# Four output stores of the first chunk issued behind the next batch's query transposes

## The chip, the cores and the metric

The kernel runs on one core of a Trainium2 chip. The metric is device time in microseconds (us), the median of several runs. A core has five engines with instruction queues of their own: TensorE (PE in the profile; its weight loads are the row PEld), VectorE (DVE), ScalarE (ACT), GpSimd (POOL) and SyncE (SP). [...] In this kernel the transfers issued by SyncE and those issued by GpSimd are two separate queues.

## The reference

Eight batches of eight heads, 576 positions and 64 elements a head go through an attention whose softmaxes are taken apart: q is normalised over the head's elements, k over the positions, and the product of k and v is a 64x64 matrix per head. The result, 512 wide, goes through a layer norm and a two-layer network with a hidden width of 2048, and is added to it.

```python
q_s = exp(q - max(q, -1)); q_s /= sum(q_s, -1) + 1e-09
k_s = exp(k - max(k, 2));  k_s /= sum(k_s, 2) + 1e-09
kv = einsum('bhsd,bhse->bhde', k_s, v)
x = einsum('bhsd,bhde->bhse', q_s, kv)      # then to (8, 576, 512)
xn = (x - mean(x)) / sqrt(var(x) + 1e-06) * g_ln
out = x + maximum(xn @ w_ch1, 0) @ w_ch2    # w_ch1 512x2048, w_ch2 2048x512
```

## The kernel before

**Chunks.** The work is cut into nine chunks. Chunk c (0 to 7) is the first 512 of the 576 positions of batch c, as four tiles (t = 0 to 3) of 128 rows; position 4p + t lies on partition p of tile t. Chunk 8 (`C9`) holds the last 64 positions of all batches. For chunk c the network is run (`mlp_steps(c)`) while the attention of chunk c + 1 and the loads and exponentials of batch c + 2 go on beside it.

**Order.** The order of the instructions on each engine is written out by hand. `run(main, side)` goes through a list of TensorE steps with weights; a side task has a due place, and it is emitted when the sum of the weights gets there. So in chunk 1's list, `second_side()` (lines 857 to 880), a task at 9.3 comes ahead of one at 9.4, and on each engine the instructions stand in the order in which the tasks emit them. Each queue is executed in that order: an instruction that waits holds back all that stands behind it on its engine.

**The network.** Chunk 0 uses plain products (`mm1_part`, `mm2_stream`). From chunk 1 on the second layer, and from chunk 2 on the first layer too, uses seven products of half blocks in place of eight (`mm2_fast`, `mm1_fast`), with sums and differences of blocks prepared beforehand. For the first layer these are `tq`, four differences of blocks of the transposed, normalised chunk `xnT`. `sum_x` (lines 233 to 245) makes them on GpSimd in eight instructions, two for each of the four; the second needs the first, the fourth the second. TensorE uses the first in product 5, the second in product 6, the third in product 7 and the fourth in product 4 (line 716).

**Transposes.** `xnT` and `eqT` (the exponentials of q, transposed) are made by DMA transposes on SyncE's queue from batch 2 on (`dma_T`, line 253): `xn_T(2, 0, 2)` and `xn_T(2, 2, 2)` at 60 and 77 of chunk 1's list, `eq_T(2)` at 9.2, `eq_T(3)` at 85.

**Loads.** Batch b needs `qt`, `kt` (1 MB each), `ktr` (the last 64 keys, two small loads), `vt` and `vr`. Weights and the loads of batches 1 and 2 are issued by GpSimd, one behind the other (`load_behind`). From batch 3 on, q and k are issued by SyncE (`load_batch`, line 1063) and v by GpSimd (`load_v`, line 139), which also converts v to bf16 on the way. Batch 3's query load has one more dependency: `load_batch(3, (2,), eqTs[2][...])` at 9.3 of chunk 1's list has GpSimd copy four elements out of `eqT` of batch 2 into the place where `qt` will land (line 1070). The copy waits for the transposes of batch 2, and SyncE's load of `qt` waits for the copy; the `kt` load, the `ktr` loads and the transposes of chunk 2's `xn` stand behind it on SyncE's queue.

**Stores.** `y_out` (line 480) makes chunk 0's output rows on VectorE, one tile of 128x512 in fp32 at a time, in the buffer `ot` (four buffers), and issues the store to `out` on GpSimd at once (line 490), 256 KB each. Chunks 1 to 7 do the same in `y_quarter` (line 570, store at line 581).

On GpSimd's queue the order around the end of chunk 0 is thus: batch 2's loads, the four stores of chunk 0, the copy out of `eqT`, `load_v(3)`, then `sum_x(2)`.

Of the kernel before, what the change touches and what calls it, by code (L numbers as in the profile page):

```python
# [20 lines left out]
def kernel(  # L21
# [16 lines left out]
    nc = tc.nc  # L38

    B, H, S, D = q.shape  # L40
# [3 lines left out]
    T = 4  # L44
    SM = P * T
# [55 lines left out]
    def main_src(x, b, h0, hn):  # L101
        return x[b, h0 : h0 + hn, 0:SM, :].rearrange("h (p t) d -> p h (t d)", t=T)
# [19 lines left out]
    def load_krem(eng, b):  # L122
        for half in range(2):
            eng.dma_start(
                raws[b][3][SR * half : SR * half + SR],
                k[b, 4 * half : 4 * half + 4, SM:S, :].transpose([1, 0, 2]),
            )
# [3 lines left out]
    def cast_v(b, j, eng=None):  # L131
        hs = slice(4 * j, 4 * j + 4)
        dst = vm[:, b % 2, :, hs, 0:D].rearrange("p t h d -> p h t d")
        if eng is nc.scalar:
            nc.scalar.copy(dst, vts[b][:, hs])
        else:
            nc.vector.tensor_copy(out=dst, in_=vts[b][:, hs])

    def load_v(b):

        vts[b] = mlp.tile([P, H, T, D], BF16, tag="vt", name="vt", bufs=1)
        nc.gpsimd.dma_start(vts[b].rearrange("p h t d -> p h (t d)"), main_src(v, b, 0, H))
        if b == 1:
            load_krem(nc.gpsimd, b)
        for half in range(2):
            hs = slice(4 * half, 4 * half + 4)
            nc.gpsimd.dma_start(
                vr[SR * half : SR * half + SR, b % 2, hs, 0:D],
                v[b, hs, SM:S, :].transpose([1, 0, 2]),
            )  # L150
# [15 lines left out]
    def exp_k(b, j, hn=2):  # L166
        kt = raws[b][0]
        if j == 0:
            eks[b] = att.tile([P, T, H, D], BF16, tag="ek", name="ek", bufs=1)
        hs = slice(2 * j, 2 * j + hn)  # L170
        nc.scalar.activation(
            eks[b][:, :, hs, :].rearrange("p t h d -> p h t d"), kt[:, hs], AF.Exp
        )

    def prep_kvrem(b):
        nc.scalar.activation(ekr[:, b % 2], raws[b][3], AF.Exp)
# [9 lines left out]
    def exp_q(b, j, hn=2):  # L186
        if j == 0:
            new_eq(b)
        hs = slice(2 * j, 2 * j + hn)
        nc.scalar.activation(  # L190
            eqs[b][0][:, :, hs, :].rearrange("p t h d -> p h t d"),
            raws[b][2][:, hs], AF.Exp,
        )
# [11 lines left out]
    def reduce_q(c, t, tn=1):  # L205
        ts = slice(t, t + tn)
        nc.vector.reduce_sum(eqs[c][1][:, ts], eqs[c][0][:, ts], axis=AX.X)  # L207
# [49 lines left out]
    def eq_T(c):  # L257
        dma_T(eqTs[c], eqs[c][0].rearrange("p t h d -> p (t h d)"), 0, T)
# [103 lines left out]
    def kv_all(b):  # L362
        kv_mm(b, range(T + 1))
        kv_out(b)

    def start_x(c):
        xs[c] = (
            mlp.tile([P, T, DM], BF16, tag="x", name="x"),
            mlp.tile([P, T, 6], FP32, tag="st", name="st"),
            mlp.tile([P, T, DM], BF16, tag="xn", name="xn", bufs=1),  # L370
            mlp.tile([P, T, 2], FP32, tag="mv", name="mv"),
        )
        xnTs[c] = mlp.tile([P, T, KO1, P], BF16, tag="xnT", name="xnT")
# [21 lines left out]
    def square_sum(c, t):  # L395
        x, _, _, mv = xs[c]
        nc.scalar.activation(  # L397
            scrap, x[:, t], AF.Square, bias=mv[:, t, 0:1], scale=-float(DM),
            accum_out=mv[:, t, 1:2],
        )  # L400
# [26 lines left out]
    def rstd_op(c):  # L427
        mv = xs[c][3]
        lnv = sml.tile([P, T], FP32, tag="lnv", name="lnv")
        rstds[c] = mlp.tile([P, T], FP32, tag="rstd", name="rstd")  # L430
        nc.scalar.activation(
            lnv, mv[:, :, 1], AF.Ln, bias=eps_ln, scale=1.0 / DM ** 3
        )
        nc.scalar.activation(rstds[c], lnv, AF.Exp, scale=-0.5)
# [24 lines left out]
    def mm1_part(c, m, t0, tn, ko):  # L459
# [13 lines left out]
        if m % 2 == 1 and at + tn == 2 and ko == KO1 - 1:  # L473
# [3 lines left out]
            else:  # L477
                nc.scalar.activation(dst, ph, AF.Relu)

    def y_out(c, t, pc, cols=slice(0, 512), eng=None):  # L480
        if cols.start == 0:
            hbox["ot"] = outp.tile([P, DM], FP32, tag="ot", name="ot")
        ot = hbox["ot"][:, cols]
        nc.vector.scalar_tensor_tensor(
            ot, in0=pc, scalar=rstds[c][:, t : t + 1], in1=xs[c][0][:, t, cols],
            op0=ALU.mult, op1=ALU.add,
        )
        eng = eng or nc.gpsimd
        if c < B:
            eng.dma_start(  # L490
                out[c, 0:SM, :].rearrange("(p t) n -> p t n", t=T)[:, t, cols], ot
            )
        else:
            for half in range(2):
                eng.dma_start(
                    out[2 * t + half, SM:S, cols], ot[64 * half : 64 * half + 64]
                )

    def mm2(c, t, ko):
        if ko == 0:  # L500
            hbox["pc"] = mm_ps.tile([P, DM], FP32, tag="m", name="pc")
        nc.tensor.matmul(
            hbox["pc"], hbox["h"][:, ko, t, :], w2_sb[:, ko, :],
            start=(ko == 0), stop=(ko == KO2 - 1),
        )
        if ko == KO2 - 1:
            y_out(c, t, hbox["pc"])
# [12 lines left out]
    def quarter_w2(i, g):  # L520

        ks = slice(4 * g, 4 * g + 4)
        rows = [w2_sb[:, 8 * g + odd : 8 * g + 8 : 2, :] for odd in range(2)]
        (b11, b12), (b21, b22) = [(r[:, :, 0:DH2], r[:, :, DH2:DM]) for r in rows]
        t1, t2, t3, t4 = [w2_q[:, n, ks, :] for n in range(4)]
        dst, x, y = ((t1, b12, b11), (t3, b22, b12), (t2, b22, t1), (t4, b21, t2))[i]
        nc.vector.tensor_sub(out=dst, in0=x, in1=y)
# [312 lines left out]
    def recip_q(c):  # L840
        nc.vector.reciprocal(eqs[c][2], eqs[c][1])
# [15 lines left out]
    def second_side():  # L857

        s = [(p, lambda i=i: quarter_w2(i, 1)) for i, p in enumerate((13, 16, 44, 46))]
        s += [(8, lambda: xn_pT(1, 2, nc.scalar)), (12, lambda: xn_pT(1, 3, nc.vector))]  # L860
        s += [(3, lambda: exp_q(2, 0, 4)), (9, lambda: exp_q(2, 2, 4)), (9.2, lambda: eq_T(2))]
        s += [(42, lambda: square_sum(1, 2)), (67, lambda: square_sum(1, 3)), (71, lambda: rstd_op(1))]
        s += [(9.3, lambda: load_batch(3, (2,), eqTs[2][0:1, T - 1, NP - 1, 0:4])), (31, lambda: load_batch(3, (0,)))]
        s += [(18 + 2 * j, lambda j=j: cast_v(2, j)) for j in range(2)]
        s += [(9.4, lambda: load_v(3))]
        s += [(93 + j, lambda j=j: cast_v(3, j)) for j in range(2)]
        s += [(15 + 3 * t, lambda t=t: reduce_q(2, t, 2)) for t in (0, 2)]
        s += [(36, lambda: recip_q(2))]
        s += [(18, lambda: exp_k(2, 0, 4)), (22, lambda: exp_k(2, 2, 4)), (26, lambda: prep_kvrem(2))]
        s += [(41, lambda: kv_all(2))]  # L870
        s += [(46, lambda: start_x(2))]
        for t, (p0, p1) in enumerate(((52, 54), (57, 59), (62, 65), (70, 74))):
            s += spread([lambda t=t, i=i: po_mm(2, t, i) for i in range(NP)], p0, p1)
            s += [(p1, lambda t=t: x_fast(2, t)), ((73, 82, 88, 94)[t], lambda t=t: square_sum(2, t))]
        s += [(60, lambda: xn_T(2, 0, 2)), (77, lambda: xn_T(2, 2, 2)), (100, lambda: rstd_op(2))]
        s += [(75, lambda: exp_q(3, 0, 4)), (79, lambda: exp_q(3, 2, 4)), (85, lambda: eq_T(3))]
        s += [(97, lambda: exp_k(3, 0, 4)), (108, lambda: exp_k(3, 2, 4)), (113, lambda: prep_kvrem(3))]
        s += [(p, lambda i=i: sum_w1(i, 1)) for i, p in ((2, 28), (3, 30))]
        s += spread([lambda i=i: sum_x(2, i) for i in range(4)], 95, 108)
        return s  # L880
# [39 lines left out]
    def xn_pT(c, t, eng):  # L920
        pe_T(xnTs[c], xs[c][2][:, t], t, eng, None if c else g_col)
# [141 lines left out]
    def load_batch(b, parts=(2, 0), after=None):  # L1063

        alloc(b, parts)
        for which in parts:
            if after is None:
                nc.vector.memset(raws[b][which][0:1, 0, 0, 0:1], 0.0)
            else:
                nc.gpsimd.tensor_copy(out=raws[b][which][0:1, 0, 0, 0:4], in_=after)  # L1070
        for which in parts:
            load_main(nc.sync, b, which, 0, H)
        if 0 in parts:
            load_krem(nc.sync, b)
# [100 lines left out]
```

## Time and profile before

| | us |
|---|---|
| median of 3 runs | 265.17 |
| lowest, highest | 264.51, 265.96 |
| the profiled execution's own time | 264.17 |
| its span, first to last instruction | 261.9 |
| TensorE's matmuls busy | 255.9 (98%) |
| VectorE busy | 216.8 (83%) |
| ScalarE busy | 180.8 (69%) |
| GpSimd busy | 77.5 (30%) |

The profile is one execution. Its page gives busy times, the chain of work that ended last, and the costliest groups of instructions by line. The trace behind it answers further questions: time lines (start, duration, engine, line, what is written from what, and in brackets the idle time ahead with what ended it), waits (engine, line and the instruction waited for, total, number and longest), the time from a transfer's issue to its landing, and stretches (a stretch's length, then for PE, PEld, DVE, ACT and POOL the busy time and, in brackets, the number of instructions, then TensorE's granted clock, a measure of the DMA engines' load, and GB/s moved). PEq and SPq mean an engine's own queue of issues.

A store or load is "issued" when the engine hands it over; it "lands" when its completion is signalled. TensorE's matmuls are pipelined, so that the duration of one is longer than the distance to the next: 0.109 us for 256 columns.

### The profile page before, as it was taken

To read this page: it belongs to the slowest core of one execution; us is meant where nothing else is said; L and a number is where in the kernel's file an instruction comes from. 1 tells how busy PE (TensorE), PEld (TensorE's weight loads), DVE (VectorE), ACT (ScalarE), POOL (GpSimd) and SP (SyncE) were. 2 spreads that over 40 slices of the span, in tenths; PEclk is the share of its full clock that TensorE was granted. 3 is DMA by queue.
4 is the path that set the end of the run, shared out by engine and by line. 5 is a ranking of instruction groups with operands and counts; after the bars stand their busy time and mean duration, and the time that the engine had idled before them with its cause. 6 is when DMAs were issued, how large, how long until landed. Compare 5 with 4: busy or idle time off the path is not lost.

```text
span 261.9 us, 6813 instructions
## 1 busy us (share of the span) xinstructions
PE 255.9 (98%) x2700; PEld 217.5 (83%) x2700; DVE 216.8 (83%) x480; ACT 180.8 (69%) x356; POOL 77.5 (30%) x128
## 2 busy tenths in 40 slices
PE   8899999999999999999999999999999999999993
PEld 6689755766888998899889988998899888888883
DVE  5667777988889997989798979897989889977873
ACT  4787581897966788678867886788688378437400
POOL 8661237203049008500850085008200300030000
PEclk9999999999999999999999999999999999999999
DMA  6999999997987994899489969997805610421014
GB/s 220 255 202 206 336 218 301 286 165 234 210 151 230 298 145 87 239 290 142 86 247 284 139 86 253 276 146 142 260 5 78 176 73 1 83 95 68 0 43 120
DMA packets 69879, 45.00 MB, mean 172 GB/s; under 512 B 41492, under 2 KB 66072, under 8 KB 69848
## 3 DMA queue, kind: packets, MB, share of 16 engines
q0 software_dynamic: 20352, 22.29, 39.2%
q1 hardware_dynamic: 48896, 21.76, 39.0%
q10 hardware_dynamic: 600, 0.53, 0.6%
q8 instruction: 21, 0.34, 0.5%
q14 instruction: 10, 0.08, 0.1%
HBM read 36.70 MB, written 9.44 MB: 176 GB/s over the span
## 4 chain that ended last, share of the span: by engine, by line
PE 95%; DMA 2%; SPq 1%; ACT 0%; issue 0%; DVE 0%
PE ba L564 21%; PE bx L716 19%; PE bb L716 9%; PE ph L467 8%; PE bb L564 5%; PE be L564 5%; PE bc L564 5%; PE pc L513 5%; PE bc L716 5%; PE ph L452 3%; PE po L383 3%; DMA kt<-in_k_dram 2%; PE pkv L347 2%; PE ptr L900 1%; PE xt L320 1%; SPq L953 1%
## 5 line engine op out<-in xcount | busy, mean ns | idle before, releaser
L564 PEld LDWEIGHTS <-hs 128*128 128x128 bf16 x512 | 49.6, 98 | 5.6
L716 PEld LDWEIGHTS <-w_q 128*128 128x128 bf16 x448 | 43.2, 98 | 4.9
L564 PEld LDWEIGHTS <-hT 128*128 128x128 bf16 x392 | 37.4, 98 | 4.4
L245 POOL TENSOR_TENSOR tq<-xnT 128x256 bf16<-128x256 bf16 x20 | 12.9, 661 | 77.6 <-DMA xnT<-xn 46.4
L716 PEld LDWEIGHTS <-w1g 128*128 128x128 bf16 x336 | 32.2, 98 | 3.9
L564 PE MATMUL ba<-w_q,hs 128*128 128x256 bf16 x256 | 31.7, 273 | 0.0
L716 PE MATMUL bx<-tq,w_q 128*128 128x256 bf16 x224 | 29.0, 273 | 0.0
L581 POOL DMA_DIRECT2D out_dram<-ot x28 | 15.3, 555 | 46.0 <-DVE ot L575 46.0
L397 ACT ACTIVATE scrap<-x,mv 128x512 bf16<-128x512 bf16 x36 | 26.0, 721 | 1.8 <-DVE x L413 1.4
L413 DVE SCALAR_TENSOR_TENSOR x<-po,rq 128x512 bf16<-128x512 f32 x34 | 23.3, 686 | 1.4 <-PE po L383 1.2
L740 ACT COPY bc<-bx 128x512 f32<-128x512 f32 x28 | 15.2, 596 | 13.0 <-PE bx L716 13.0
L758 ACT ACTIVATE hT<-bc 128x512 bf16<-128x512 f32 x28 | 15.3, 595 | 12.2 <-PE bc L716 12.2
L747 DVE TENSOR_TENSOR bb<-bx,s 128x512 f32<-128x512 f32 x28 | 18.2, 694 | 6.7 <-ACT s L744 6.7
L207 DVE TENSOR_REDUCE zq<-eq 128x16 f32<-128x1024 bf16 (+1 forms) x20 | 20.8, 1052 | 2.4 <-ACT eq L190 2.1
L544 DVE TENSOR_TENSOR hs<-hT 128x1024 bf16<-128x1024 bf16 x32 | 20.9, 675 | 0.8 <-ACT hT L758 0.5
L758 ACT ACTIVATE hT<-bb 128x512 bf16<-128x512 f32 x28 | 15.2, 595 | 8.2 <-PE bb L716 8.2
L750 DVE TENSOR_TENSOR hT<-bx,s 128x512 bf16<-128x512 f32 x28 | 18.0, 685 | 2.8 <-PE bx L716 2.8
L383 PE MATMUL po<-kv_sb,eqT 128*128 128x128 bf16 x120 | 20.2, 219 | 0.0
L589 ACT COPY s<-ba 128x512 f32<-128x512 f32 x15 | 8.7, 578 | 11.9 <-PE ba L564 7.3
L564 PE MATMUL ba<-w_sb,hT 128*128 128x256 bf16 x128 | 16.7, 273 | 0.0
L564 PE MATMUL bb<-w_q,hs 128*128 128x256 bf16 x128 | 16.5, 273 | 0.0
L190 ACT ACTIVATE eq<-qt 128x1024 bf16<-128x1024 f32 x14 | 14.6, 1056 | 1.7 <-DMA qt<-in_q_dram 1.7
(146 smaller groups left out, 538.4 us busy)
## 6 DMA issues: line engine op xcount, KB each, us to landing
out_dram<-ot POOLq DMA_DIRECT2D x32, 256.0 KB, 5.9
qt<-in_q_dram SPq DMA_DIRECT2D x5, 1024.0 KB, 7.0
kt<-in_k_dram SPq DMA_DIRECT2D x5, 1024.0 KB, 14.5
vt<-in_v_dram POOLq DMA_DIRECT2D x7, 512.0 KB, 14.1
qt<-in_q_dram POOLq DMA_DIRECT2D x2, 1024.0 KB, 12.9
kt<-in_k_dram POOLq DMA_DIRECT2D x2, 1024.0 KB, 13.9
w_sb<-in_moe_w_ch_dram POOLq DMA_DIRECT2D x3, 512.0 KB, 16.0
kt<-in_k_dram SPq DMA_DIRECT2D x4, 288.0 KB, 5.2
```

The lines of the kernel that those rows point to most:

```text
L207: nc.vector.reduce_sum(eqs[c][1][:, ts], eqs[c][0][:, ts], axis=AX.X)
L383: nc.tensor.matmul(pobox["p"][:, i * P : i * P + P], eqTs[c][:, t, i, :], kv_sb[:, c, i, :], start=True, stop=True,)
L397: nc.scalar.activation(scrap, x[:, t], AF.Square, bias=mv[:, t, 0:1], scale=-float(DM), accum_out=mv[:, t, 1:2],)
L413: nc.vector.scalar_tensor_tensor(x[:, t].rearrange("p (h d) -> p h d", h=H), in0=pobox[c, t].rearrange("p (h d) -> p h d", h=H), scalar=1. ...
L467: nc.tensor.matmul(ph[:, m % 2, at : at + tn], (w1g if c else w1_sb)[:, ko, m * P : (m + 1) * P], xnTs[c][:, t0 : t0 + tn, ko, :], start=( ...
L544: nc.vector.tensor_tensor(out=dst, in0=x, in1=y, op=op)
L564: nc.tensor.matmul(dst, lhsT, rhs, start=first and (own or t == 0) and k == 0, stop=k == KH - 1, skip_group_check=True)
L581: nc.gpsimd.dma_start(out[c, 0:SM, :].rearrange("(p t) n -> p t n", t=T)[:, t], ybox[c, t])
L716: nc.tensor.matmul(dst[:, q], lhsT, rhs, start=first and q == 0 and ko == 0, stop=ko == 1, skip_group_check=True)
L747: nc.vector.tensor_tensor(out=at[g, "b"], in0=at[g, "x"], in1=at[g, "s"], op=ALU.add)
L750: nc.vector.tensor_tensor(out=h_out(g, 1, 1), in0=at[g, "x"], in1=at[g, "s"], op=ALU.add)
L758: nc.scalar.activation(h_out(g, odd, half), at[g, name], AF.Relu)
```

## The change

Chunk 0's four stores are no longer issued in `y_out`. The tiles are kept in a list, and a new task `store_late` in chunk 1's list issues them, at 9.4. `load_v(3)` moves from 9.4 to 9.5. The four stores so stand behind the copy out of `eqT` (9.3) and ahead of `load_v(3)` on GpSimd's queue; the copy is the only instruction that they are moved past. The other engines' queues keep their instructions in the same order.

```diff
+    late = []
+
     def y_out(c, t, pc, cols=slice(0, 512), eng=None):
...
         eng = eng or nc.gpsimd
-        if c < B:
+        if c == 0:
+            late.append((t, ot))
+        elif c < B:
             eng.dma_start(
                 out[c, 0:SM, :].rearrange("(p t) n -> p t n", t=T)[:, t, cols], ot
             )
...
+    def store_late():
+        for t, ot in late:
+            nc.gpsimd.dma_start(
+                out[0, 0:SM, :].rearrange("(p t) n -> p t n", t=T)[:, t, :], ot
+            )
...
         s += [(9.3, lambda: load_batch(3, (2,), eqTs[2][0:1, T - 1, NP - 1, 0:4])), (31, lambda: load_batch(3, (0,)))]
         s += [(18 + 2 * j, lambda j=j: cast_v(2, j)) for j in range(2)]
-        s += [(9.4, lambda: load_v(3))]
+        s += [(9.4, store_late), (9.5, lambda: load_v(3))]
```

## The prediction

> **What bounds the kernel now.** I read the busy times first, then the waits, then the time lines of the engines around the moved stores, then the DMA engines in stretches of equal meaning. All times are microseconds from the span's start.
>
> From the page's first part, and from the waits of TensorE's weight loads between 60 and 258:
>
> ```profile
> PE 255.9 (98%) x2700; PEld 217.5 (83%) x2700; DVE 216.8 (83%) x480; ACT 180.8 (69%) x356; POOL 77.5 (30%) x128
> PEld L347 <- issue: 1.1, 5, 0.2
> PEld L390 <- issue: 0.4, 2, 0.2
> ```
>
> TensorE waits for no other engine and no transfer from 60 to the end; the same question for its matmuls gave no row at all. The stream is as dense before that: from 63.71 to 76.22 stand 112 matmuls of 256 columns (0.109 each, the pace of 16 in 1.75) and 5 of 128 columns (0.055), 12.5 in 12.51; from 55.33 to 63.71, 32 of 512 columns (0.218), 12 of 128 and batch 2's 40 key-value products (0.76) make 8.4 in 8.38. So nothing placed after 48 can make this execution shorter, and anything that makes TensorE wait once adds its whole length: chunk follows chunk every 26.21 (76.22, 102.43, 128.64) and no later gap could take it back.
>
> The question is thus only whether something comes late. SyncE's and GpSimd's queues around the change, from the time line (start, duration, what, and in brackets the idle time ahead with its releaser):
>
> ```profile
> 52.77 4.29 SPq L253 DMA_TRANSPOSE eqT<-eq  x1
> 59.27 0.40 SPq L117 DMA_DIRECT2D qt<-in_q_dram  x1
> 59.85 0.44 SPq L117 DMA_DIRECT2D kt<-in_k_dram  x1
> 60.39 2.30 SPq L124 DMA_DIRECT2D ktr<-in_k_dram  x2
> 64.26 8.09 SPq L253 DMA_TRANSPOSE xnT<-xn  x2
> ```
>
> ```profile
> 47.40 1.22 POOL L490 DMA_DIRECT2D out_dram<-ot  x2 [1.73 <-DVE ot L484]
> 50.71 0.54 POOL L490 DMA_DIRECT2D out_dram<-ot  x1 [2.09 <-DVE ot L484]
> 52.61 0.54 POOL L490 DMA_DIRECT2D out_dram<-ot  x1 [1.36 <-DMA vt<-in_v_dram]
> 59.06 0.18 POOL L1070 CAST qt<-eqT 1x4 f32<-1x4 bf16 x1 [5.91 <-DMA eqT<-eq]
> 60.30 0.91 POOL L142 DMA_DIRECT2D vt<-in_v_dram  x1 [1.06 <-DVE w_q L527]
> 75.32 1.30 POOL L245 TENSOR_TENSOR tq<-xnT 128x256 bf16<-128x256 bf16 x2 [12.83 <-DMA xnT<-xn]
> 76.59 1.28 POOL L245 TENSOR_TENSOR tq<-xnT,tq 128x256 bf16<-128x256 bf16 x2
> ```
>
> The four stores leave at 47.4 to 52.6. The query transposes of batch 2 land at 58.97; the cast at 59.06 waits for them and releases the loads of batch 3 on SyncE. Behind those loads, on the same queue, stand the transposes of chunk 2's xn. The second lands at 75.25 (issue at 68.4, 6.8 to landing), and GpSimd waits for it. TensorE's use of tq:
>
> ```profile
> 76.22 1.04 PE L716 MATMUL bx<-xnT,w1g 128*128 128x256 bf16 x8
> 77.09 1.04 PE L716 MATMUL bb<-tq,w_q 128*128 128x256 bf16 x8
> 77.96 1.04 PE L716 MATMUL bx<-tq,w_q 128*128 128x256 bf16 x8
> ```
>
> The second pair of tq instructions ends at 77.87 and TensorE takes it at 77.96: **a margin of 0.09**. Two chunks later the pair ends at 128.04 for 130.39, a margin of 2.3. Chunk 2's xn transposes are the tight place of the kernel.
>
> The DMA engines from the issue of the query load to the landing of the second key remainder, for batches 3, 4 and 5, and the quiet 2 us between transposes and loads (last column GB/s):
>
> ```profile
> 59.30:71.20 11.90, 11.90 (x102) 9.04 (x101) 10.79 (x24) 10.14 (x23) 2.18 (x3) 1.00 1.04 238
> 78.50:95.10 16.60, 16.60 (x194) 14.83 (x192) 15.23 (x31) 12.68 (x24) 6.21 (x10) 1.00 1.09 242
> 104.70:121.80 17.10, 17.10 (x199) 15.28 (x198) 15.68 (x33) 12.70 (x24) 3.92 (x7) 1.00 1.08 237
> 59.00:61.00 2.00, 2.00 (x13) 1.05 (x12) 1.69 (x3) 1.80 (x5) 0.87 (x2) 1.00 0.15 18
> ```
>
> The first row has no output stores in it, the other two have four, of the same size and on the same queue (issued at 80.3 and 104.2). The rate is the same 240 GB/s; the stretch is 4.7 and 5.2 longer. The changed kernel makes batch 3's loads like those of batches 4 and 5.
>
> **The change part by part.**
>
> *Stores taken away from 47.4 to 57.2.* DVE and ACT work there waits for none of them. What gains are the query transposes: issued at 52.77, when ACT ends its exponentials (unchanged), and landing 6.2 later beside the last stores (the fourth lands at 57.2). In quiet stretches the same transposes took 4.3 (issues at 97.12 and 123.34). So they land near 57.1 to 57.2, **1.8 earlier**; bounds 0 (something else held them) and 1.9. TensorE's first use of eqT at 60.51 waits for nothing today, so this is worth nothing by itself. The cast and SyncE's qt and kt follow it (the kt load also waits for DVE's memset at 57.67, which is over by 57.73): the loads start near 57.5 instead of 59.27.
>
> *Stores put between the cast and load_v(3) on GpSimd.* Four issues at 0.55 are 2.2 of GpSimd, as at 80.33; the queue moved past is only the cast. The load of v leaves near 59.6 to 60.7 instead of 60.30, so its issue time hardly changes. GpSimd's next work is tq, 14 later: free. The ot buffers are next written by DVE at 73.11; stores issued by 59.6 with the 7.7 to 9.3 that those of chunk 1 needed land by 69: free.
>
> *1.05 MB more beside the q, k and v loads.* This is the price. From the nearest rows, batches 4 and 5, it is 4.7 to 5.2; by bytes at the stretch's own rate 1.05 MB / 240 GB/s = 4.4; at the highest rate of any microsecond that I looked at (406 GB/s at 86 to 87) it would be 2.6. The rows of batches 4 and 5 moved 0.14 to 0.17 MB more than stores account for (4.02 and 4.05 against 2.83 MB), so I take the byte price, **4.3**, with 2.6 and 5.2 as ends. [...]
>
> *Sum.* The key remainder, the last load ahead of the xn transposes on SyncE's queue, lands 4.3 - 1.8 = 2.5 later. The transposes end 4.0 behind it today (71.2 to 75.25) and 4.0 behind it for batch 4 (95.1 to 99.1), so xnT comes 2.5 late, tq 2.5 late, and TensorE stalls **2.5 - 0.1 = 2.4** at 77 to 78. Two more things come late there, beside it and not on top. k of batch 3 lands 14.6 to 15.9 after the query issue (batches 4 and 5), 72.1 to 73.4, and ACT, which takes it at 71.66 today, waits 0.4 to 1.7 ahead of the copy at 73.03 that product 4 at 74.47 needs: up to 0.9 of the stall may show there. v lands at 73.7 to 74.7, so DVE's cast at 72.43 comes 1.3 to 2.3 late, with the output sums and the PSUM banks behind it. All three are dates that TensorE meets in order; the latest sets the end.
>
> From the profiled execution's 264.17 (span 261.9 and 2.3 around it) that gives 266.6. That execution is 1.0 faster than the median of the runs shown, 265.17 (lowest 264.51). I put the same stall on the median: **267.6**. Ends of the terms: stall 2.6 - 1.9 - 0.1 = 0.6 to 5.2 - 0 - 0.1 = 5.1, so 265.8 to 270.3.
>
> **The rivals.**
>
> *The stores are nearly hidden.* They start into the quiet 2 us after the transposes (18 GB/s at 59 to 61) and move at the peak rows' 400 GB/s. Then the stall is 0.6 or less: 265.2 to 265.8. For it: the quiet stretch exists. Against: it follows the cast in batches 4 and 5 too, where it did not shorten the stretch. Chance 0.20. [...]
>
> *Faster.* The transposes and q, k come 1.8 earlier and the stores take less than that from SyncE's queue, so xnT lands before 75.25. It decides only if 1.05 MB cost under 1.8, 580 GB/s, above any row. Even then this execution cannot shorten, as TensorE's stream is dense; only runs that wait today could, and the 1.0 by which the median exceeds the profile is all the times show: 264.2. Chance 0.08, and 0.05 for more than 0.5% (below 263.8).
>
> *The stall costs the clock too.* Behind the last matmul, at 257.8, the granted clock's mean is 0.67 over 260 to 261.9, as half speed from about 260.65 on: 2.9 after TensorE fell idle. A stall of one piece longer than that (transposes not earlier, stores at 5.2) would go on at half speed for a while; half speed for the 1.25 that the tail shows loses 0.6. With a stall of 4.2 that is 270.0. [...] Chance 0.07.
>
> **How the numbers follow.** The stall of about 2.4 has 0.65, hidden 0.20, faster or nothing 0.08, the clock 0.07. About 0.5% (1.3 us) is what a measurement of this kernel can tell from no change. Slower by more: 0.65 and 0.07, a little of the first lying under 1.3 and a little of hidden above it, 0.73. Within: 0.22. Faster: 0.05. The range leaves out the lower half of hidden's end and the far end of the clock: 265.2 to 270.0.
>
> **What would show it.** In the changed kernel's trace: eqT of batch 2 lands near 57.1 (wrong if still near 59); the stores issue at about 57.4 to 59.6 with v right behind; the stretch from qt's issue to the second ktr landing is near 16 instead of 11.9 at an unchanged 240 GB/s (wrong if the rate rises over 300); tq starts near 77.8 instead of 75.32; TensorE has a gap of about 2.4 in total between 74 and 79, and chunks repeat every 26.2 after it. The prediction fails if tq starts by 75.4 all the same.

## The result

The changed kernel takes 266.28 us (median of 22 runs, 265.04 to 268.76) where the kernel before takes 264.56 (median of 22 runs, 263.83 to 265.96). The ratio is 1.0068 with a 95% interval from 1.0048 to 1.0088: slower by about 1.8 us. A second comparison gave 1.0068 again, from 1.0046 to 1.0091. The ratio is above the half per cent which the prediction set as the bound of what can be told from no change; both intervals begin just under it, and neither holds 1.

The profiled execution took 265.47 us, its span is 263.2 (before: 264.17 and 261.9). Time lines of SyncE and GpSimd in the changed kernel, in the form shown for the kernel before (start, duration, what, idle time ahead and its releaser; lines behind 507 of the program are moved by 10):

```profile
52.41 2.77 SPq L253 DMA_TRANSPOSE eqT<-eq  x1
57.44 0.40 SPq L117 DMA_DIRECT2D qt<-in_q_dram  x1
58.01 0.45 SPq L117 DMA_DIRECT2D kt<-in_k_dram  x1
58.57 5.01 SPq L124 DMA_DIRECT2D ktr<-in_k_dram  x2
63.75 10.33 SPq L253 DMA_TRANSPOSE xnT<-xn  x2
```

```profile
56.95 0.47 POOL L1080 CAST qt<-eqT 1x4 f32<-1x4 bf16 x1 [11.99 <-DMA eqT<-eq]
57.49 2.18 POOL L505 DMA_DIRECT2D out_dram<-ot  x4
60.30 0.91 POOL L142 DMA_DIRECT2D vt<-in_v_dram  x1 [0.63 <-DVE w_q L537]
76.73 1.29 POOL L245 TENSOR_TENSOR tq<-xnT 128x256 bf16<-128x256 bf16 x2 [14.24 <-DMA xnT<-xn]
77.99 1.29 POOL L245 TENSOR_TENSOR tq<-xnT,tq 128x256 bf16<-128x256 bf16 x2
```

The query transposes of batch 2 land at 56.9 (issue at 52.41 and 4.5) instead of 59.0. The loads of batch 3 start 1.8 earlier. v leaves at the same 60.30. But the second transposes of chunk 2's `xn` land at 76.6 (issue at 70.1, 6.5 to landing) instead of 75.2, and `tq` begins at 76.73 instead of 75.32. TensorE's time line at chunk 2's start:

```profile
74.22 1.91 PE L574 MATMUL ba<-w_q,hT 128*128 128x256 bf16 x16
75.96 1.04 PE L726 MATMUL bx<-xnT,w1g 128*128 128x256 bf16 x8
78.07 1.03 PE L726 MATMUL bb<-tq,w_q 128*128 128x256 bf16 x8 [1.07 <-POOL tq L245]
79.33 1.03 PE L726 MATMUL bx<-tq,w_q 128*128 128x256 bf16 x8 [0.22 <-ACT s L754]
80.29 0.70 PE L347 MATMUL pkv<-vm,ek 128*64 128x65 bf16 x32
```

Eight matmuls of 256 columns take 0.87 (77.09 to 77.96 in the kernel before), so `bb` could have begun at 76.83 and began at 78.07, when the first pair of `tq` was ready (78.02). The next product waited until 79.33 for the second pair (ready at 79.28); that this row names ScalarE's copy, which ended at almost the same moment, changes nothing (in the kernel before this product began at 77.96, and the same copy ended later, at 78.4). From there on the stream is dense again. Among the waits of the weight loads from 60 on, which were two lines of "issue" before, stands this one:

```profile
PEld L726 <- DVE ot L585: 0.7, 1, 0.7
```

It is a second late arrival at the same place: VectorE, held by the load of v (it waited 2.6 for it instead of 1.0), freed the bank of `bb` late. Which of the two decides is asked below.

**A measure without the scatter of the start.** TensorE enters chunk 1 at 47.89 in the profile before and at 47.52 in the profile after; over all profiles of this study it is 47.1 to 49.4. This difference arises before that entry, where the kernels differ by one store alone. So I count from that entry (the first matmul of line 467 behind chunk 0's last products). In the kernel before, the key-value products at chunk 2's start begin 31.04 behind it without any gap; what is over 31.04 is the gap. In the changed kernel it is 80.29 - 47.52 = 32.77: **a gap of 1.73**.

### The profile page after: what moved, and what is told of

It is laid out like the page before. It is cut to its first block, busy times and chain, and to the rows that moved or that the text cites. A ratio compares the mean times of both kernels' runs of the same rounds, so it can differ in the third digit from the quotient of the medians.

```text
span 263.2 us, 6810 instructions
## 1 busy us (share of the span) xinstructions
PE 256.3 (97%) x2697; PEld 217.9 (83%) x2700; DVE 216.5 (82%) x480; ACT 181.0 (69%) x356; POOL 77.4 (29%) x128
## 4 chain that ended last, share of the span: by engine, by line
PE 77%; DMA 16%; DVE 2%; POOL 2%; issue 1%; ACT 1%; POOLq 0%; ACTq 0%
PE bx L726 18%; PE ba L574 18%; PE bb L726 9%; DMA ktr<-in_k_dram 7%; DMA w_raw<-in_moe_w_ch_dram 5%; PE bc L726 5%; PE be L574 5%; PE bc L574 5%; PE bb L574 5%; PE ph L467 3%; PE ph L452 3%; DMA xnT<-xn 2%; DMA v<-in_v_dram 2%; PE po L383 2%; PE pkv L347 2%; DVE hs L554 1%
## 5 line engine op out<-in xcount | busy, mean ns | idle before, releaser
L245 POOL TENSOR_TENSOR tq<-xnT 128x256 bf16<-128x256 bf16 x20 | 12.9, 660 | 79.0 <-DMA xnT<-xn 47.8
L591 POOL DMA_DIRECT2D out_dram<-ot x28 | 15.3, 556 | 46.0 <-DVE ot L585 46.0
L768 ACT ACTIVATE hT<-bc 128x512 bf16<-128x512 f32 x28 | 15.3, 594 | 12.7 <-PE bc L726 12.7
L599 ACT COPY s<-ba 128x512 f32<-128x512 f32 x15 | 8.7, 579 | 11.9 <-PE ba L574 7.3
L754 ACT COPY s<-bb 128x512 f32<-128x512 f32 x28 | 15.5, 622 | 1.0 <-PE bb L726 1.0
## 6 DMA issues: line engine op xcount, KB each, us to landing
kt<-in_k_dram SPq DMA_DIRECT2D x5, 1024.0 KB, 14.2
```

What stands on the lines that cost most here:

```text
L591: nc.gpsimd.dma_start(out[c, 0:SM, :].rearrange("(p t) n -> p t n", t=T)[:, t], ybox[c, t])
L754: nc.scalar.copy(at[g, "s"], at[g, "b"])
L768: nc.scalar.activation(h_out(g, odd, half), at[g, name], AF.Relu)
```

## The experiments

All short diffs are against the changed kernel, except where it is said.

**The stores left out.** The task `store_late` is removed, so that these four tiles of the output are never written.

```diff
-        s += [(9.4, store_late), (9.5, lambda: load_v(3))]
+        s += [(9.5, lambda: load_v(3))]
```

> The changed kernel without its four held stores: chunk 0's first 512 rows are never written, so this time leaves 1.05 MB of output out. Theory (the stores beside batch 3's loads delay the xn transposes): batch 2's query transposes land near 57.0 as in the changed kernel, the loads run as in the kernel before but 1.8 us earlier, ktr lands near 69.3, xnT near 72.5, TensorE has no gap between 74 and 80, and the time is that of the kernel before or up to 0.4 us less (264.1 to 264.6). Rival (the change costs elsewhere, for instance by the later place of load_v or by the order on GpSimd, not by the bytes): a gap of 1 us or more stays, 265.5 or more.

Measured: 263.58 us, ratio to the kernel before 0.9957 (0.9931 to 0.9983). TensorE's time line has no idle time:

```profile
76.45 1.04 PE L726 MATMUL bx<-xnT,w1g 128*128 128x256 bf16 x8
77.33 1.04 PE L726 MATMUL bb<-tq,w_q 128*128 128x256 bf16 x8
78.20 1.04 PE L726 MATMUL bx<-tq,w_q 128*128 128x256 bf16 x8
```

Here `xnT` lands 26.4 behind the entry (27.3 before), and the key-value products begin at 31.05. So the loss does not come from the place of the v load in the queue: it needs the stores beside the loads. The time is 0.8 below the median of the kernel before, more than the 0.4 expected at most, which suggests that the kernel before waits in some of its executions. Two dates were missed: the second key remainder lands at 72.4 and `xnT` at 74.5, where 69.3 and 72.5 were expected. Without any store beside it the stretch is 14.2 here, longer than in the kernel before; v leaves 0.3 behind `qt` here and 1.0 there.

**Does the kernel before wait there too?** It was profiled twice more, unchanged.

> The kernel before, unchanged, profiled once more. The kernels without the stores in this place and with two of them behind v had medians 0.4 to 0.8 us below it, though the first profile of it shows no gap at chunk 2's start. Theory (xnT's margin is 0.09 us, so that other executions of the kernel before wait there): xnT lands up to 1.5 us later than 27.3 us after TensorE enters chunk 1, and the key-value products start as much later than 31.04. Rival (the difference is made before chunk 1): 27.3 or less and 31.0 to 31.1 again.

> The same as b_again1, a third profile of the kernel before: with a margin of 0.09 about half of such profiles should show a gap of 0.1 to 1.5 us at chunk 2's start if the theory holds, and none if not.

Measured: the second profile of the kernel before has a gap of 1.64 (entry 47.14, key-value products at 79.82), the third none (entry 47.80, products at 78.84). The second's time line at chunk 2's start:

```profile
75.47 1.04 PE L716 MATMUL bx<-xnT,w1g 128*128 128x256 bf16 x8
77.60 1.03 PE L716 MATMUL bb<-tq,w_q 128*128 128x256 bf16 x8 [1.09 <-POOL tq L245]
78.86 1.03 PE L716 MATMUL bx<-tq,w_q 128*128 128x256 bf16 x8 [0.22 <-ACT s L744]
```

It is the same wait as in the changed kernel. The query transposes and the stores met in a different way in each of these executions: the transposes took 6.2, 7.6 and 5.3 to land, and the loads of batch 3 started 11.4, 12.9 and 10.5 behind the entry. In every profile of a kernel that does not issue the last two stores beside the transposes, the start is 9.9 to 10.1.

**VectorE's wait for v taken away.** The two casts of v stand behind chunk 1's output sums instead of ahead of them.

```diff
-        s += [(93 + j, lambda j=j: cast_v(3, j)) for j in range(2)]
+        s += [(200 + j, lambda j=j: cast_v(3, j)) for j in range(2)]
```

> The changed kernel with batch 3's two v casts on VectorE moved from ahead of chunk 1's output sums to behind them, so that VectorE no longer waits for the v load there. Two late arrivals ended within 0.1 us of each other in the changed kernel: tq (78.0) and the output sums that free PSUM banks (77.3 to 78.1). Theory (xnT sets the end): the gap stays 1.5 to 1.8 us, 266.0 to 266.4. Rival (VectorE held by the v load sets it): the gap falls to 0.3 us or less, 264.6 to 264.9.

Measured: 266.25 us, ratio 1.0062 (1.0035 to 1.0088), as the changed kernel. VectorE's wait is gone from the list and the gap is not:

```profile
PE bb L726 <- POOL tq L245: 1.5, 1, 1.5
```

The gap is 2.07, a little above the 1.5 to 1.8 expected; `xnT` landed 28.7 behind the entry, which alone would make 1.4, and the first pair of `tq` took 1.95 instead of 1.29. So VectorE was late beside `xnT`, not the cause.

**The added load without the earlier start.** The four stores stay in their old places and are issued a second time where the changed kernel has them.

```diff
         if c == 0:
             late.append((t, ot))
-        elif c < B:
+        if c < B:
```

> The kernel before, with its four stores in their old places, and the same four stored a second time where the changed kernel has them. This takes the earlier transposes away and leaves the added load. Theory: the loads start at 59.3 as before, the stretch from qt's issue to the second ktr landing grows from 11.9 to about 16.8, xnT lands near 78.6, TensorE's gap is about 3.3 us: 267.5 to 268.2, about 1.5 us above the changed kernel. Rival (the earlier start of the loads was worth nothing): the time of the changed kernel, 266.0 to 266.6.

Measured: 267.72 us, ratio 1.0111 (1.0071 to 1.0150), 1.4 above the median of the changed kernel (1.1 by the two ratios). `xnT` landed 29.9 behind the entry and the gap is 2.62, in three pieces, one of them ahead of chunk 2 where ScalarE waited for k. The expected `xnT` near 78.6 was met (78.8); the gap came out at 2.6 instead of 3.3, since this execution entered chunk 1 0.9 later than the first profile of the kernel before. The earlier start is worth something by the run times, as forecast. The trace bears out less of it: the loads start 10.5 behind the entry here and 9.9 or 10.0 in the changed kernel, and v leaves 3.5 behind `qt` instead of 2.9 and 3.2, so that the start is not all that differs.

**v first.** `load_v(3)` and the four stores change places on GpSimd.

```diff
-        s += [(9.4, store_late), (9.5, lambda: load_v(3))]
+        s += [(9.4, lambda: load_v(3)), (9.5, store_late)]
```

> The changed kernel with load_v(3) ahead of the four stores on GpSimd. v leaves 2 to 3 us earlier and lands near 71, the stores leave near 60 to 62. The bytes beside SyncE's loads are the same. Theory (shared DMA engines delay xnT): xnT still lands between 76.0 and 77.0, gap 1.2 to 1.8 us, 265.8 to 266.4. Rival (v's lateness on VectorE sets the end): gap 0.3 us or less, 264.6 to 264.9.

Measured: 264.54 us, ratio 0.9997 (0.9972 to 1.0022), against the time that my theory expected and near that of the rival. But the trace does not bear the rival out: v was there in time (68.8), and the gap was 0.87, not 0.3 or less, with `tq` as its releaser:

```profile
76.20 1.04 PE L726 MATMUL bx<-xnT,w1g 128*128 128x256 bf16 x8
77.56 1.03 PE L726 MATMUL bb<-tq,w_q 128*128 128x256 bf16 x8 [0.33 <-POOL tq L245]
78.81 1.03 PE L726 MATMUL bx<-tq,w_q 128*128 128x256 bf16 x8 [0.22 <-ACT s L754]
```

> All four stores behind v once more. Its profile showed a gap of 0.9 us where its median was that of the kernel before. If the order on GpSimd recovers most of the loss, 0.999 to 1.003 again and a gap of 0 to 0.9 us; if the first median was chance, 1.004 or more.

The second time: 265.26 us, ratio 1.0048 (1.0030 to 1.0066), again a gap of 0.88. By its time this run falls where the expectation calls the first median chance, by its gap where it does not. So v first is worth half of the loss or more in the traces; the two times disagree with each other, and which is nearer stays open. What fell is my assumption that only the number of bytes counts. k landed 11.9 and 12.0 behind the issue of qt, against 14.8 and 15.6 in the two profiles of the changed kernel.

**Two stores held instead of four.** Tiles 0 and 1 are stored at once, as before.

```diff
-        if c == 0:
+        if c == 0 and t >= 2:
             late.append((t, ot))
```

> Only the stores of tiles 2 and 3 are held; tiles 0 and 1 are stored at once, as in the kernel before. Half the bytes beside batch 3's loads, and most of the earlier query transposes. Theory (price by bytes in that stretch, 3.9 us for 1.05 MB from the changed kernel's trace): transposes of batch 2 land near 57.3, the loads start near 57.8, the stretch is near 14.9, xnT lands near 75.1, 27.2 us after TensorE enters chunk 1, and TensorE's gap is 0.3 us or less: 264.2 to 264.8. Rival (any held store ahead of v costs the same, because it is the place in the queue that counts): a gap of 1.2 us or more, 265.6 or more.

> Two stores held ahead of v once more. Its profile had as long a stretch as with four (16.8 us) and a gap of 1.3 us, its median only 0.7 us over the kernel before. If the price goes by bytes, the stretch is near 15 here and the gap 0 to 0.5 us, time ratio 1.000 to 1.003; if two cost as much as four, the stretch is near 16.8 again, the gap 1.3 or more, ratio 1.005 or more.

Measured: ratios 1.0018 (0.9994 to 1.0043) and 1.0021 (1.0000 to 1.0043), gaps 1.34 and 1.56. k landed 15.3 and 15.6 behind qt's issue, as late as with four stores. The stretch to the second ktr landing of the first of the two, with the DMA rate in the last column, beside that of the changed kernel and that of v first:

```profile
58.26:75.10 16.84, 16.84 (x161) 12.82 (x154) 13.13 (x30) 13.70 (x31) 3.26 (x5) 1.00 1.09 211
```

```profile
57.44:74.20 16.76, 16.76 (x160) 12.84 (x154) 12.63 (x29) 14.16 (x32) 4.37 (x7) 1.00 1.06 240
```

```profile
57.78:72.60 14.82, 14.82 (x145) 11.17 (x138) 12.91 (x30) 13.07 (x29) 4.28 (x7) 1.00 1.06 266
```

Half of the bytes take the same time at a lower rate, and the same bytes in another order take 2 us less at a higher one. The rate is not a constant of the stretch. In the traces, two stores ahead of v cost nearly as much as four, as the rival had it; the run times lie where the theory of bytes had them and show a smaller loss than with four. Both profiles are of executions above their median (265.89 and 265.26, medians 264.91 and 264.96). About half of the first gap and over two thirds of the second come ahead of chunk 2: ScalarE waited 1.4 and 1.8 for k, and TensorE then 0.5 and 1.0 for ScalarE.

What the order changes can be read from the two queues in the first 8 us behind qt's issue (packets, MB, and their share of the time of the core's 16 DMA engines; q1 is SyncE's queue, q0 GpSimd's). The changed kernel, two held ahead of v, and v first:

```profile
q1 hardware_dynamic: 1253, 1.27, 52.2%
q0 software_dynamic: 220, 0.75, 27.9%
```

```profile
q1 hardware_dynamic: 1252, 1.27, 57.5%
q0 software_dynamic: 240, 0.55, 22.8%
```

```profile
q1 hardware_dynamic: 1526, 1.55, 62.1%
q0 software_dynamic: 627, 0.32, 29.0%
```

With two stores ahead of v SyncE's queue moves as little of q and k as with four. In these windows a packet of a store is 4 KB (184 packets of 2 to 8 KB in the changed kernel's window hold nearly all of q0's 0.75 MB), one of q or k 1 KB (1.27 MB in 1253 packets) and one of v 0.5 KB (0.32 MB in 627 with v first). Between 6 and 10 us behind qt's issue the two queues send as many packets each beside v (670 and 672) and similar numbers beside the stores (394 and 339); for SyncE's queue that is 0.69 MB with v first and 0.40 MB in the changed kernel. After 12 us it has moved 2.19 MB with v first and 1.81 in the changed kernel, where q and k together are 2.10. In the second profile of v first k lands at 69.6 and the stores behind it, the first at 72.2 and the last at 74.3; in the changed kernel the last store lands at 68.4 and k at 72.2.

**Two stores, behind v.**

```diff
-        if c == 0:
+        if c == 0 and t >= 2:
             late.append((t, ot))
...
-        s += [(9.4, store_late), (9.5, lambda: load_v(3))]
+        s += [(9.4, lambda: load_v(3)), (9.5, store_late)]
```

> Tiles 2 and 3 held and issued behind load_v(3), tiles 0 and 1 stored at once. If the price of a store behind v is half of that ahead of it, as the run with v first suggests (1.9 against 3.9 for four), it is 1.0 for two, less than the 1.8 that the loads gain at their start: xnT lands 26.5 to 27.0 us after TensorE enters chunk 1, earlier than in the kernel before (27.4), no gap, and the time is 0.3 to 0.7 us below the kernel before, as without the stores at all: 263.6 to 264.1. Rival (the kernel before rarely waits at this place): no difference, 264.2 to 264.6.

> The two stores behind v once more, for its time against the kernel before: 0.9975 was measured, its interval ending at 0.9999. If the gain is real, 0.995 to 0.999 again; if it was chance, 0.999 to 1.002. In the trace no gap, key-value products 31.0 to 31.2 us after TensorE enters chunk 1.

Measured: 263.80 and 263.76 us, ratios 0.9975 (0.9951 to 0.9999) and 0.9982 (0.9962 to 1.0002), gaps 0.08 and 0. That is the best of the kernels with all output, 0.4 to 0.6 below the medians of the kernel before in the same comparisons. `xnT` lands 27.4 and 27.0 behind the entry, not at the 26.5 to 27.0 expected: on the edge of the margin, about as in the first profile of the kernel before. One of the two intervals holds 1, so the gain is likely and not settled.

**The changed kernel once more.**

> The changed kernel once more on the same chip, to compare with two held stores: stretch 16 to 17 us, gap 1.4 to 2.2 us, ratio 1.005 to 1.009.

Measured: 1.0068 (1.0046 to 1.0091). This profile is of an execution of 267.11, the longest of this run, with a gap of 2.51, above the 1.4 to 2.2 expected. Here TensorE's waits name VectorE and ScalarE, not `tq`:

```profile
PE bb L726 <- DVE ot L585: 1.1, 2, 0.9
PE ba L574 <- ACT s L599: 0.9, 1, 0.9
```

k, v and `xnT` are all late by similar amounts (k landed 15.6 behind qt's issue, v at 75.9). The first pair of `tq` was ready at 79.63, 0.11 ahead of the start of `bb`.

**All profiles together.** Start: issue of batch 3's qt behind the entry into chunk 1. Then k's landing and the landing of the second half of `xnT`, both behind that issue; `xnT` behind the entry; the gap.

| kernel (stores beside the loads) | start | k | xnT | xnT from entry | gap |
|---|---|---|---|---|---|
| before, three profiles (none) | 11.4, 12.9, 10.5 | 10.4, 10.9, 10.3 | 15.9, 16.0, 16.0 | 27.3, 29.0, 26.5 | 0, 1.64, 0 |
| left out (none) | 10.1 | 11.6 | 16.3 | 26.4 | 0 |
| two behind v, twice | 10.0, 9.9 | 11.6, 11.9 | 17.5, 17.1 | 27.4, 27.0 | 0.08, 0 |
| four behind v, twice | 9.9, 9.9 | 11.9, 12.0 | 18.3, 18.3 | 28.2, 28.2 | 0.87, 0.88 |
| two ahead of v, twice | 9.9, 10.1 | 15.3, 15.6 | 18.8, 18.8 | 28.7, 28.9 | 1.34, 1.56 |
| four ahead of v: changed, twice | 9.9, 10.0 | 14.8, 15.6 | 19.2, 19.8 | 29.1, 29.8 | 1.73, 2.51 |
| four ahead of v, casts late | 9.9 | 14.7 | 18.8 | 28.7 | 2.07 |
| four in both places | 10.5 | 15.4 | 19.5 | 29.9 | 2.62 |

The gap is the fifth column less 27.35, and none where that is negative, within 0.1 in every row but that of the late casts, where `tq` itself took 0.66 longer. In seven of the eight kernels TensorE loses what `xnT` is late. Where TensorE waits earlier for ScalarE, held by k, the sum is still that of `xnT`, which comes last; what late k would cost with `xnT` in time no run shows. The span less the entry and the gap is 214.0 within 0.05 in every profile but that of the stores in both places (214.25): what a kernel wins or loses lies in these two.

## Why the prediction was right

The forecast was slower, by 2.4 us, 267.6 with a range of 265.2 to 270.0. The mechanism held: the stores beside batch 3's loads delay `xnT`, and TensorE waits for `tq`. Measured were 1.7 and 2.2 us more than the medians of the kernel before in the two comparisons (266.28 against 264.56, 266.29 against 264.12), 1.73 and 2.51 in the two traces. Of the 1.3 by which 267.6 is too high, 0.6 is the base: 265.17 was the median of three runs, 264.56 that of 22. The other 0.7 is the stall, 2.4 against the 1.7 between the medians. Part of that is that the kernel before waits too: its medians lie 0.4 to 0.8 above those of the kernels whose profiles show next to no gap (264.35 against 263.58, 264.22 against 263.80), so that as an estimate the stall itself is some 2.1 to 2.5.

*Nothing to gain in a dense stream, all to lose at the tight place.* Right, and it decided the sign. The margin of 0.09 was real: without it the kernel before waits, as its second profile did (1.64).

*The transposes 1.8 earlier.* In the profiles compared, qt starts 1.83 earlier, and the transposes take 1.8 less (4.5 instead of 6.2), as forecast. That qt gains all of it is luck: 0.29 more passes between their landing and qt's issue, and they were issued 0.36 earlier, as TensorE entered chunk 1 0.37 earlier. Behind the entry qt starts 1.5 earlier. It is no constant either: against the three profiles of the kernel before the start behind the entry is 0.5 to 3.0 earlier. What the change does is to make it 9.9 or 10.0.

*v's issue unchanged, GpSimd free, ot free.* Right: v leaves at 60.30 as before, and the last of the stores landed at 68.4 (59.13 and 9.2), ahead of VectorE's first use at 74.31.

*The price, 4.3.* Here the working had a reading wrong and a term too high. The landing of the second key remainder was misread in the kernel before: it is issued at 62.1 and lands at 72.2, not 71.2. The stretch before was thus 12.9 and not 11.9, and the transposes ended 3.0 behind it, not 4.0. In the date of `xnT` the two errors cancel (11.9 + 4.0 and 12.9 + 3.0). But the price from the rows of batches 4 and 5 was 1.0 too high: 16.6 and 17.1 less 12.9 are 3.7 and 4.2, not 4.7 and 5.2 (for batch 4 the trace records the landing of the first remainder only, 94.3, so that 95.1 is an estimate). In the changed kernel the stretch is 16.8, and the transposes end 2.3 behind it. The price of the stores was 3.9 in the stretch, and the tail, which the sum took as unchanged, gave back 0.7: 3.2 for `xnT`. With a start 1.8 earlier `xnT` comes 1.4 late, where 2.5 was forecast, and `tq` starts at 76.73, not near 77.8; TensorE had entered 0.37 earlier and had 0.09 of margin: 1.4 + 0.37 - 0.09 = 1.7, as measured. The second profile of the changed kernel has a price of 3.9 and a gap of 2.51. So the forecast stall of 2.4 lies between the two traces, and that it does is in part the scatter of the price and of the start.

*"The rate is the same 240 GB/s."* Wrong as a rule. It is 240 in the changed kernel, as forecast, but 225 in the true stretch of the kernel before, 211 with two stores, and 266 with v first. The price goes by bytes only behind v (1.1 to 1.5 for two and 2.3 for four, from `xnT` behind qt's issue and against the kernel before; 0.3 to 0.4 less each against the kernel without the stores); ahead of v the first two cost 2.8 and all four 3.2 to 3.9. With stores ahead of v k landed 14.7 to 15.6 behind qt's issue, 3 to 4 later than without the stores (11.6), and with stores behind v 11.6 to 12.0; SyncE's queue moved 1.24 to 1.29 MB in its first 8 us beside the 4 KB packets and 1.53 to 1.65 with the stores behind v. Why two stores take as much from it there as four stays open.

*Late k and late v beside it, not on top.* Right in the first profile (ScalarE waited 0.8 for k, VectorE 2.6 for v); for v the late casts show it. For k no run separates it: in the second profile of the changed kernel, with two held ahead of v and with the stores in both places, 0.5 to 1.1 of the gap shows at ScalarE, where up to 0.9 was forecast. In the second profile of the changed kernel `tq` and the bank that VectorE frees came within 0.2 of each other.

*The rivals.* Hidden: the stores did issue into the quiet 2 us, and the price was 3.2 and 3.9, above the 2.6 of this rival. Faster: it is real for a kernel whose stores cost less (left out, or two behind v), and its size was nearly right: 1.0 was forecast from the median to a run that does not wait, and 0.4 to 0.8 was measured. The bound of 1.8 on the price, beyond which it fails, was passed by every version with all output but that with two stores behind v. The clock: no stretch of either profile shows less than 1.00 between 76 and 82; the longest single piece of a gap in them was 1.24 (76.83 to 78.07), where the prediction read 2.9 off the tail. In the kernel before 0.50 stands over 260.65 to 261.9, with no matmul behind it; that a longer stall would go on at half speed was an estimate from this tail, which no run shows.

## What to carry to other kernels

The stores that were taken out of the way of one late transfer went beside another: the loads started 1.8 earlier, and `xnT` came 3.2 later behind that start. Find the tightest date behind the new place of a transfer before moving it, and subtract the start that is won from the price that is paid. Where TensorE's stream is dense, read margins instead of busy shares; a margin of 0.1 in one profile can mean that some executions wait already, and here the second profile of the same kernel showed it, with a gap of 1.64. The order within one queue mattered here as much as the bytes: four stores behind v left a gap of 0.87 and 0.88, four ahead of it 1.73 and 2.51, two ahead of it 1.34 and 1.56. So what nobody waits for is worth trying behind what somebody waits for.

## What was not expected of the hardware

The same 1.05 MB of stores beside the same loads took 16.8 at 240 GB/s ahead of v and 14.8 at 266 GB/s behind it, and half of them ahead of v took 16.8 at 211. k's landing behind qt's issue has two ranges, 10.3 to 12.0 and 14.7 to 15.6, and which one holds went with whether stores stood ahead of v, not with how many (two or four). In the first 8 us behind that issue SyncE's queue moved 1.24 to 1.29 MB with two or with four stores ahead of v, 1.53 to 1.65 with stores behind it, and 1.66 and more with none. The query transposes of batch 2, 4.3 to 5.0 long in every kernel that holds the last two stores back, took 5.3 to 7.6 beside them in the three profiles of the kernel before and with the stores in both places.
